# First GLU pass: product B11 of f tiles 1 to 13 by a nested seven-product scheme, and its background work placed anew

## The chip, the cores and the metric

The kernel runs on one core of a Trainium2 chip. The metric is device time in microseconds (us); the version before has a median of 2357.12 us over three runs (2354.83 to 2357.94). Engines: PE multiplies matrices, PEld is its weight load, DVE (vector), ACT (scalar) and POOL (GpSimd) work elementwise, SP issues DMAs. A row of the profile such as `L144 PE MATMUL` names the line of the kernel file that issued the instruction.

## What is computed

```python
x  = A_x                                  # 2048 x 1024, fp32
xn = layernorm(x)
q, k, v = split(xn @ wqkv)                # 1024 -> 3 x 1024, 32 heads of 32
phi(y) = concat(softmax(y @ w_phi), softmax(-(y @ w_phi)))    # per head
o  = phi(q) (phi(k)^T v) / (phi(q) sum(phi(k)) + 1e-6);  s = o @ wo
h  = sigmoid(xn @ w_gate) * (xn @ w_up)   # 1024 -> 3584, cut into 14 f tiles
out = x + s * silu(h @ w_down)
```

## The kernel before

**Products.** Each large product is cut in 2 x 2 and done with seven products instead of eight (a Strassen scheme in Winograd's form): B11, B21, B22 and T1 to T4 name the seven, and the sums of operand quarters that they need. An fp32 operand is split into a high and a low fp32r part by `split`: an ACT cast (L135) and a DVE subtraction (L136). `mm3` (L144 to L146) then issues three 128x512 matmuls, high by high, high by low and low by high, for one product of 128 rows of the contraction. A unit of work over one f tile ("glu op") fills PSUM banks 0 to 3 with 4 x 4 x 3 = 48 matmuls.

**The program order.** `ops` lists the work. The first projection chunk comes first, its opening written out by hand. GLU pass 0 follows: for each of 14 f tiles the ops B11 and B21, 28 of them. Then come the second projection chunk, GLU pass 1 (T2, T3, T4 of each f), pass 2 (T1, B22), the down product, and the attention with its output. The seven products of one f thus lie in three passes; between these, banks are copied out by ACT and kept in memory, and seeded or added again later.

**A nest.** In pass 2 the op T1 of f+1 is itself done by seven smaller products inside op B22 of f, for f = 1 to 12. `nest` fills banks 4 to 7 with six matmuls each for seven inner products (`product`), in place of 48, and between them runs the four quarters of the plain op (`plain`, 12 matmuls each, banks 0 to 3): 7 x 6 + 48 = 90 matmuls. Inner results pass from bank to bank by ACT: bank 4 to bank 5 (T2 adds to it), bank 5 to bank 6 (T3), bank 6 to bank 4 (T4). Bank 7 goes through a buffer in SBUF and is added by DVE (`added`). The finished quarters are added to what earlier passes left (`result`) and copied into banks 0 to 3, where the next plain op continues. The weights of a nest need four POOL sums of 128x256 (L530 to L533) and six splits instead of two, one of them half as large; `prep` does the splits ahead into a ring of eight slots, freed by `used()`.

**Background work.** `tick()` counts steps of the program and `later(n, f)` runs f at n ticks on: transfers, sums and normalisation for other stages. A glu op has one tick. `begin_pass` places the work: in pass 0 `x_stats`, `x_scales` and `x_rows` (the norm of the second half of x), four `x_pair` (they apply the norm by two 128x1024 DVE operations per `x_apply`, L849, and make POOL sums L254 and L290), and 16 `q_steps` (softmax of the query features: DVE L661, L662, L671, L672, L680, L681, and an ACT Exp of 128x1024, L675). Exp and the Sigmoid of the gate (L1425) use different ACT tables, so that an `ACT_TABLE_LOAD` stands ahead of each when they alternate. `wd_sums` are groups of four POOL sums of the down weights (L880 to L883): six groups in pass 1 (`WD_B`), four in pass 2 (`WD_C`). Instructions keep program order on each engine, so an instruction that waits holds up all behind it there.

**Attention in pass 1.** `kv_products` (L733) are small PE matmuls behind DVE's `k_low` (L727), which they follow by a fixed number of ticks.

Of the kernel before, what the change touches and what calls it, by code (L numbers as in the profile page):

```python
# [49 lines left out]
def hedgehog_glu_kernel(  # L50
# [103 lines left out]
    def later(n, f, *a):  # L154
        plan.setdefault(clock[0] + n, []).append((f, a))
# [15 lines left out]
    def tick():  # L171

        clock[0] += 1
        with behind():
            glu_group()
            nest_load()
            if not nests:
                glu_load(len(ops) - 1)
# [104 lines left out]
    xsets = (((53, 54), ((8, 9), (10, 11))), ((0, 1), ((2, 3), (26, 27))))  # L283
# [53 lines left out]
    o_split = Ring((54, 36, 37, 38))  # L337
# [38 lines left out]
    def folded(which, k, n, ps):  # L376
        f, r = FB[n][0], fraw[which][4 * k + n]
        for g in range(4):
            gs = slice(g * P, (g + 1) * P)
            nc.tensor.matmul(ps[:, gs], r[:, gs], bd[:, 4 * f + g], start=True, stop=True)  # L380
# [37 lines left out]
    ops += [("glu", 0, f, i) for f in range(NJ) for i in PASSES[0]]  # L418
# [10 lines left out]
    gr = Ring((41, 42, 39, 40))  # L429
# [4 lines left out]
    WD_B, WD_C = range(6), range(6, 10)  # L434
    last_raw, raw_free, spare, groups, made_sums = [], deque(), [], deque(), {}
    for f in FLY:
        groups.extend((f, s) for s in range(2))
        if 0 <= f - 4 < len(WD_B):
            groups.append((WD_B[f - 4], None))
    nests, nested = deque(k for k in range(1, NJ - 1)), {}  # L440

    def glu_load(n):
# [7 lines left out]
        if p == 0:  # L450
            r = gr.next()
            last_load[:] = [nc.sync.dma_start(whole(r), src).ins]
            wraw[n] = halves(r)
            return True
        if (p, f, i) == (1, 0, T2):
            raw_free.extend(halves(41, 42, 39, 40))
# [60 lines left out]
    def nest_load():  # L517

        if not nests or len(raw_free) < 6 or ops.index(("glu", 2, 1, T1)) not in wraw:
            return  # L520
        k = nests.popleft()
        ra, rb, rc, rd, gate, up = [raw_free.popleft() for _ in range(6)]
        for s, o in enumerate((ra, rb)):
            nc.sync.dma_start(o, wg_d[summed.index(T1), k + 1, :, s * HB:(s + 1) * HB])
        for s, o in enumerate((gate, up)):
            last_load[:] = [nc.sync.dma_start(o, wg_d[summed.index(B22), k, :, s * HB:(s + 1) * HB]).ins]
        lo, hi = slice(0, 256), slice(256, HB)

        def sums():
# [4 lines left out]
            nested[k] = rc, ra, gate, rb, rd, up  # L534
# [25 lines left out]
    def prep():  # L560
# [18 lines left out]
        if kind == "nest" and what not in nested:  # L579
# [3 lines left out]
        if kind == "nest":  # L583
            s = len(ready[n])
            src, cols = nested[what][s], slice(0, 256 if s == 4 else HB)
# [14 lines left out]
        if c:  # L600
            release(src)
# [201 lines left out]
    def x_stats(n):  # L803
        xt = x_load(CTT + n, xstat.next())
        later(5, x_moments, n, xt)
# [11 lines left out]
    def x_rows(q):  # L817

        rows = tps.next()
# [6 lines left out]
    def x_pair(u):  # L826

        xs, temps = xsets[u % 2]
        for th in range(2):
            n = 4 * th + u  # L830
            x_in(xs[th], temps[th], n)
            for w in range(2):
                later(4 + 2 * th + w, x_apply, xs[th], n, w)
            later(6 + 2 * th, x_keep, xs[th], temps[th], n, th, u)
            later(9 + 2 * th, outer_keep, n, temps[th])
        later(12, lambda: x_sums(halves(xs[0]), halves(xs[1])))
        later(15, lambda: x_sums_keep(u, halves(xs[0]), halves(xs[1])))

    def x_in(slot, temps, n):
        nc.sync.dma_start(whole(slot), xT[n])  # L840
# [10 lines left out]
    def x_keep(slot, temps, n, th, u):  # L851
# [6 lines left out]
        outer_sums(n, halves(slot), temps)  # L858
# [82 lines left out]
    qf_raw, qf_e = Ring(halves(36)), Ring((37, 38))  # L941

    def q_steps(at, t, hb):
# [16 lines left out]
        for n, f in ((0, load), (5, first), (6, lambda: spread(hold[2], *hold[:2])), (9, lambda: exponentials(hold[1])),  # L960
                     (11, sums), (13, keep)):
# [482 lines left out]
    def begin_projection(c):  # L1444
# [9 lines left out]
        for n in range(5):  # L1454
# [539 lines left out]
```

## Time and profile before

| | us |
|---|---|
| median of three runs | 2357.12 (2354.83 to 2357.94) |
| the profiled execution's own time | 2359.33 |
| its span, first to last instruction | 2357.5 |
| PE busy in the span | 2343.1 |
| DVE / ACT / POOL busy | 1651.5 / 1181.0 / 1056.9 |

| stage (us from the span's start) | length | PE | DVE | ACT | POOL busy |
|---|---|---|---|---|---|
| first projection chunk, 0 to 286 | 286 | 282.35 | 159.92 | 147.74 | 74.72 |
| GLU pass 0, 286 to 592 | 306 | 306.00 | 188.54 | 148.03 | 122.00 |
| second projection chunk, 592 to 821 | 229 | 229.00 | 185.88 | 127.02 | 36.63 |
| GLU pass 1 and the entry of pass 2, 821 to 1345 | 524 | 523.03 | 348.16 | 284.40 | 255.58 |
| GLU pass 2 with its nests, 1345 to 1580 | 235 | 231.69 | 145.63 | 117.99 | 176.59 |
| down product, 1580 to 2110 | 530 | 530.00 | 442.84 | 236.49 | 261.56 |
| attention and output, 2110 to 2357 | 247 | 241.04 | 180.57 | 119.33 | 129.82 |

The boundaries are cut by eye, at round numbers. How to read the rows shown further on: a row of the timeline gives the start, the duration, engine, line, operation, output and inputs, and in brackets the idle time of the engine ahead of it with what ended it. Matmuls overlap, so the step from one start to the next, not the duration, is what one costs. "xN" is a count; in groups, "busy, mean" are us and ns.

### The profile page before, as it was taken

The page shows a single profiled execution, that of the slowest core. Times are in us where ns is not written, and L with a number is a line of the kernel's source. Part 1 is how long each engine was busy: PE and PEld are TensorE (multiplying, and loading weights), DVE is VectorE, ACT ScalarE, POOL GpSimd, SP SyncE. Part 2 cuts the span into 40 slices and gives each one's busy share as a digit, 9 for nine tenths or more (in the row PEclk, how much of TensorE's full clock was granted, in tenths as well). Part 3 has the DMA queues.
Part 4 walks back from the last instruction along what each step waited for, and adds up shares of the span by engine and source line. Part 5 has one row for each costly group of instructions (what it writes and reads, how often), then busy time and mean ns, then how long its engine had stood idle before and what let it go on. Part 6 is the DMA issues. An engine that isn't in the chain of part 4 may idle for free.

```text
span 2357.5 us, 32347 instructions
## 1 busy us (share of the span) xinstructions
PE 2343.1 (99%) x10900; PEld 1954.7 (83%) x10900; DVE 1651.5 (70%) x2083; ACT 1181.0 (50%) x1848; POOL 1056.9 (45%) x737
## 2 busy tenths in 40 slices
PE   9999999999999999999999999999999999999999
PEld 8888888888888888888888888788888888888887
DVE  7625557755688856568776766565999888877776
ACT  7344544455644655555555555453444444355553
POOL 0323226731132035657622677784656443424566
PEclk9999999999999999999999999999999999999999
DMA  8789989986787786878874988789877667785665
GB/s 297 258 302 358 329 316 343 376 287 205 260 271 257 251 285 231 319 263 300 279 239 153 328 269 272 231 291 351 301 255 266 225 202 246 253 284 207 204 204 180
DMA packets 300406, 633.56 MB, mean 269 GB/s; under 512 B 38096, under 2 KB 38352, under 8 KB 295632
## 3 DMA queue, kind: packets, MB, share of 16 engines
q1 hardware_dynamic: 300240, 631.51, 77.2%
q8 instruction: 85, 1.39, 0.2%
q14 instruction: 81, 0.66, 0.1%
HBM read 378.40 MB, written 252.97 MB: 268 GB/s over the span
## 4 chain that ended last, share of the span: by engine, by line
PE 93%; DMA 3%; POOL 1%; DVE 1%; issue 1%; ACT 1%; SPq 1%; POOLq 0%; DVEq 0%
PE bank L144 29%; PE bank L145 29%; PE bank L146 29%; PE bank L733 1%; PE bank L1072 1%; PE bank L1048 1%; PE bank L380 1%; DMA fc<-e_d 0%; DMA fb<-wqkT 0%; DMA x<-x 0%; DMA wf_d<-p 0%; DMA fa<-wf_d 0%; DMA fc<-w_down 0%; DMA h_d<-x 0%; PE bank L248 0%
## 5 line engine op out<-in xcount | busy, mean ns | idle before, releaser
L144 PE MATMUL bank<-x,w 128*128 128x512 f32 x2304 | 896.7, 390 | 3.3 <-ACT bank L1560 3.3
L145 PE MATMUL bank<-x,w 128*128 128x512 f32 x2304 | 897.7, 390 | 0.0
L146 PE MATMUL bank<-x,w 128*128 128x512 f32 x2304 | 896.4, 389 | 0.0
L136 DVE TENSOR_TENSOR w<-fa,w 128x512 fp32r<-128x512 f32 (+1 forms) x383 | 372.2, 978 | 356.1 <-ACT w L135 343.5
L144 PEld LDWEIGHTS bank<-x,w 128*128 128x128 f32 x2304 | 432.9, 188 | 93.0 <-ACT bank L1560 3.7
L145 PEld LDWEIGHTS bank<-x,w 128*128 128x128 f32 x2304 | 433.0, 188 | 89.5 <-DVE x L136 0.3
L146 PEld LDWEIGHTS bank<-x,w 128*128 128x128 f32 x2304 | 432.9, 188 | 89.2
L135 ACT CAST w<-fa 128x512 fp32r<-128x512 f32 (+1 forms) x383 | 263.8, 691 | 420.8 <-PE bank L145 312.0
L144 PE MATMUL bank<-w,x 128*128 128x512 f32 x708 | 277.4, 392 | 0.0
L146 PE MATMUL bank<-w,x 128*128 128x512 f32 x708 | 276.0, 390 | 0.0
L145 PE MATMUL bank<-w,x 128*128 128x512 f32 x708 | 275.9, 390 | 0.0
L146 PEld LDWEIGHTS bank<-w,x 128*128 128x128 f32 x708 | 132.9, 188 | 27.8 <-DVE x L1248 0.3
L145 PEld LDWEIGHTS bank<-w,x 128*128 128x128 f32 x708 | 133.1, 188 | 26.1
L144 PEld LDWEIGHTS bank<-w,x 128*128 128x128 f32 x708 | 133.0, 188 | 26.2
L1392 ACT COPY fc<-bank 128x512 f32<-128x512 f32 x168 | 96.9, 583 | 96.5 <-PE bank L146 49.5
L136 DVE TENSOR_TENSOR w<-fb,w 128x512 fp32r<-128x512 f32 (+1 forms) x99 | 96.3, 979 | 65.1 <-ACT w L135 64.9
L135 ACT CAST w<-fb 128x512 fp32r<-128x512 f32 (+1 forms) x99 | 60.8, 615 | 119.6 <-PE bank L145 96.7
L136 DVE TENSOR_TENSOR x<-fb,x 128x512 fp32r<-128x512 f32 (+1 forms) x86 | 95.6, 1112 | 30.9 <-ACT x L135 29.3
L1086 POOL TENSOR_TENSOR fc<-fc 128x512 f32<-128x512 f32 x32 | 48.9, 1528 | 59.3 <-DVE fc L1081 23.9
L136 DVE TENSOR_TENSOR p<-fc,p 128x512 fp32r<-128x512 f32 (+1 forms) x67 | 49.3, 747 | 32.8 <-ACT p L135 30.2
L135 ACT CAST x<-fb 128x512 fp32r<-128x512 f32 (+1 forms) x86 | 68.2, 796 | 6.1 <-DMA fb<-w_down 2.9
L311 POOL TENSOR_TENSOR fb<-fb 128x512 f32<-128x512 f32 x6 | 9.2, 1525 | 133.7 <-DMA fb<-w_gu 133.7
(399 smaller groups left out, 3614.5 us busy)
## 6 DMA issues: line engine op xcount, KB each, us to landing
m_d<-fc SPq DMA_DIRECT2D x168, 256.0 KB, 3.9
fa<-h_d SPq DMA_DIRECT2D x147, 256.0 KB, 4.3
fa<-wf_d SPq DMA_DIRECT2D x32, 1024.0 KB, 6.4
x<-m_d SPq DMA_DIRECT2D x124, 256.0 KB, 4.9
h_d<-fc SPq DMA_DIRECT2D x104, 256.0 KB, 4.2
fc<-e_d SPq DMA_DIRECT2D x48, 512.0 KB, 5.8
fc<-qkv_d SPq DMA_DIRECT2D x72, 256.0 KB, 5.0
fa<-w_gu SPq DMA_DIRECT2D x60, 256.0 KB, 4.6
```

What stands on the lines that cost most here:

```text
L135: nc.scalar.copy(o[0], src)
L136: i = nc.vector.tensor_sub(o[1], src, o[0].bitcast(F32))
L144: nc.tensor.matmul(o, a[0], b[0], start=first, stop=False, **kw)
L145: nc.tensor.matmul(o, a[0], b[1], start=False, stop=False, **kw)
L146: last_mm[:] = [nc.tensor.matmul(o, a[1], b[0], start=False, stop=last, **kw).ins]
L311: nc.gpsimd.tensor_add(a22, a21, a22)
L380: nc.tensor.matmul(ps[:, gs], r[:, gs], bd[:, 4 * f + g], start=True, stop=True)
L733: nc.tensor.matmul(kvb[g // 2][:, g % 2 * 256:g % 2 * 256 + 256], v[:, g].rearrange("p a f -> p (a f)"), ph[:, g].rearrange("p a f -> p (a ...
L1048: nc.tensor.transpose(ps[:, j * P:(j + 1) * P], e[:, k * P:(k + 1) * P], ident)
L1072: nc.tensor.matmul(ps[:, j * 256:(j + 1) * 256], kg[:, k], ph[:, a, k], start=a == 0, stop=a == 1)
L1086: nc.gpsimd.tensor_sub(o, a, b)
L1392: nc.scalar.copy(o, banks[b])
```

## The change

- **Pass 0 uses nests.** Its ops become one glu op (B11 of f = 0), 13 nests, and one glu op (B21 of f = 13). The nest of f does B21 of f as the plain op and B11 of f+1 by seven inner products. `nest`, the nest's loads, sums and splits and the x operands of the inner products (`x_nest_load`, `x_nest_sums`, `x_nest_split`) take the pass as an argument. In pass 0 a finished quarter is copied twice by ACT: to a buffer that goes to memory (L1566) and to banks 0 to 3 (L1567). A nest has six ticks where the two ops it replaces had two.
- **The end of a nest moves.** The last quarter's results (`rest`) are issued in the next op, behind its first inner product and bank copy (`finish`); `result(1)` comes earlier. This holds for both passes.
- **Background work of pass 0 is placed by the nest's ticks.** `x_rows` transposes go into bank 7 at the start of nests f = 2 to 5, `x_pair` starts at ticks 18, 30, 42, 54 with temporaries shared between its two halves, 12 instead of 16 `q_steps` run in pass 0 (one every six ticks), and the other four in pass 2.
- **Other places.** All ten early `wd_sums` groups are in pass 1 and none in pass 2. `kv_products` run one tick later except at the last t of a half. Six instead of five `glu_sums` groups are in the second projection chunk, none in pass 0. Some buffers change their slots.

```diff
-    ops += [("glu", 0, f, i) for f in range(NJ) for i in PASSES[0]]
+    ops += [("glu", 0, 0, B11)] + [("nest", 0, f, B21) for f in range(NJ - 1)] + [("glu", 0, NJ - 1, B21)]
...
-    WD_B, WD_C = range(6), range(6, 10)
+    WD_B, WD_C = range(10), ()
...
-                     (9 + wide, k_inverses), (10 + wide, k_scale), (11 + wide, k_low), (13 + 2 * wide, kv_products)):
+                     (9 + wide, k_inverses), (10 + wide, k_scale), (11 + wide, k_low), (13 + 2 * wide + (t < TT - 1), kv_products)):
...
         if p == 0:
+            copies.items = halves(51, 50)
             for n in range(CTT):
-                later(1 + n + 4 * (n > 3), x_stats, n)
-            later(19, x_scales)
-            for q in range(4):
-                later(20 + q, x_rows, q)
+                later(1 + n + n // 4, x_stats, n)
+            later(14, x_scales)
             for u in range(4):
-                later(24 + 12 * u, x_pair, u)
-            for n in range(2 * CTT):
-                q_steps(2 + 13 * n // 2, n // 2, n % 2)
-            queue2(6, glu_sums, *sums.popleft(), halves(43, 44))
+                later(18 + 12 * u, x_pair, u)
+            for n in range(12):
+                q_steps(5 + 6 * n, n // 2, n % 2)
...
-                queue2(20 + 16 * n, wd_sums, j, halves(53, 54))
+                queue2(40 + 16 * n, wd_sums, j, halves(53, 54))
+            qf_raw.items, qf_e.items = [slots[50][:, 1]], [52]
+            for n in range(4):
+                q_steps(13 + 18 * n, 6 + n // 2, n % 2)
...
+    unfinished = []
+
+    def finish():
+        while unfinished:
+            unfinished.pop()()
...
-    def nest(n, f):
+    def nest(n, p, f):
...
-            h_added(1, f, ua, q)
+            if p:
+                h_added(1, f, ua, q)
+            else:
+                h_direct(0, f, q)
 
         def result(q, ps):
 
+            if not p:
+                o = copies.next()
+                nc.scalar.copy(o, ps)
+                nc.scalar.copy(banks[q], ps)
+                nc.sync.dma_start(m_d[0, f + 1, q], o)
+                return
...
         product(B11, a, True)
         nc.scalar.copy(b, a)
+        finish()
         plain(0)
         tick()
...
-        result(3, c)
-        result(1, b)
-        gated(1)
-        uvfree.extend(va[2:])
-        h_out(1, f + 1 + NJ, va[:2])
+
+        def rest():
+            result(3, c)
+            gate(1)
+            gated(1)
+            ...
+        unfinished.append(rest)
```

The line numbers move with the change. The three bank copies of a nest are L1592 (bank 4 to 5), L1600 (bank 5 to 6) and L1612 (bank 6 to 4) in the new file, a finished quarter's copies L1566 and L1567, bank 7's copy L1579, the gate's sigmoid L1429, Exp L677, the nest's weight sums L533 to L536, the `wd_sums` L884 to L887.

On PE, in the middle of pass 0. bank_101 to bank_104 are PSUM banks 0 to 3, bank_105 to bank_108 banks 4 to 7. Before, quarter 0 of a B21 op is followed by quarter 1:

```order
L144 MATMUL bank0_101<-x5_0_92,w_0_94 128x512
L145 MATMUL bank0_101<-x5_0_92,w_0_94 128x512
L146 MATMUL bank0_101<-x5_0_92,w_0_94 128x512
L144 MATMUL bank1_102<-x1_1_718,w_0_94 128x512
L145 MATMUL bank1_102<-x1_1_718,w_0_94 128x512
L146 MATMUL bank1_102<-x1_1_718,w_0_94 128x512
```

Now quarter 0 is followed by the inner product T2 on bank 5, which starts from what ACT copied there:

```order
L144 MATMUL bank0_101<-x5_0_92,w_0_94 128x512
L145 MATMUL bank0_101<-x5_0_92,w_0_94 128x512
L146 MATMUL bank0_101<-x5_0_92,w_0_94 128x512
L144 MATMUL bank5_106<-x2_2_2078,w_0_94 128x512
L145 MATMUL bank5_106<-x2_2_2078,w_0_94 128x512
L146 MATMUL bank5_106<-x2_2_2078,w_0_94 128x512
L144 MATMUL bank5_106<-x2_2_2078,w_0_94 128x512
L145 MATMUL bank5_106<-x2_2_2078,w_0_94 128x512
L146 MATMUL bank5_106<-x2_2_2078,w_0_94 128x512
L144 MATMUL bank7_108<-x3_1_1849,w_0_94 128x512
```

Six matmuls to bank 5 stand between quarter 0 and the next inner product, on bank 7.

On ACT, in pass 0, around an Exp. Before, it stands among the copies that keep B11 (L1392) and the two gates of a B21 op:

```order
L1392 COPY fc_100<-bank_103 128x512
L135 CAST w_94<-fa_97 128x2x512
L675 ACTIVATE p_0_96<-p_0_96 128x1024
L1392 COPY fc_100<-bank_104 128x512
L1425 ACT_TABLE_LOAD
L1425 ACTIVATE fb_99<-bank_101 128x512
L1425 ACTIVATE fb_99<-bank_102 128x512
```

Now it stands in the middle of a nest:

```order
L135 CAST w_94<-fa_97 128x512
L677 ACT_TABLE_LOAD
L677 ACTIVATE p_0_96<-p_0_96 128x1024
L1579 COPY fc_100<-bank_108 128x512
L135 CAST w_94<-fa_97 128x512
L1566 COPY fc_100<-bank_105 128x512
L1567 COPY bank_101<-bank_105 128x512
L135 CAST w_94<-fa_97 128x256
L1429 ACT_TABLE_LOAD
L1429 ACTIVATE fb_99<-bank_102 128x512
L1612 COPY bank_105<-bank_107 128x512
```

Between the Exp and the copy bank 6 to 4 on the last row, on which PE's product T4 depends, stand three more copies, two casts, a table load and a sigmoid.

At a nest's end, on DVE, the x_apply (L854) and the Exp's row sums (L682) of the background now stand ahead of the nest's last additions and gate products (fb_99, fc_100 and x are buffers in SBUF, stq the row statistics):

```order
L682 TENSOR_REDUCE stq_3268<-p_0_96 128x32
L854 TENSOR_TENSOR x_1_2163<-x_1_2163,x_2_2164 128x1024
L683 RECIPROCAL stq_3268<-stq_3268 128x32
L1580 TENSOR_TENSOR bank_107<-bank_107,fc_100 128x512
L1431 TENSOR_TENSOR fb_99<-fb_99,bank_103 128x512
L136 TENSOR_TENSOR w_94<-fa_97,w_94 128x512 x2
L1580 TENSOR_TENSOR bank_106<-bank_106,fc_100 128x512
L1431 TENSOR_TENSOR fb_99<-fb_99,bank_104 128x512
```

On ACT there, a cast, a finished quarter's copies and the copy bank 6 to bank 3, which waits for the L1431 on the last row above, stand ahead of the copy bank 4 to 5 (L1592):

```order
L135 CAST w_94<-fa_97 128x512
L1579 COPY fc_100<-bank_108 128x512
L1566 COPY fc_100<-bank_106 128x512
L1567 COPY bank_102<-bank_106 128x512
L135 CAST w_94<-fa_97 128x512
L1567 COPY bank_104<-bank_107 128x512
L1592 COPY bank_106<-bank_105 128x512
```

In that chain an addition (L1580), two copies, a product (L1431) and two more copies follow one another across the two engines.

On POOL, in the second half of pass 2. Before, a `wd_sums` group (L880 to L883) lies among the weight sums of a coming nest (L530 to L533), the gate's products (L1437, L1552) and the sums of h (L1408):

```order
L880 TENSOR_TENSOR fc_100<-fc_100 128x512
L881 TENSOR_TENSOR fc_100<-fc_100 128x512
L1437 TENSOR_TENSOR fc_100<-fc_100,x_3_9538 128x512
L882 TENSOR_TENSOR fc_100<-fc_100 128x512
L1552 TENSOR_TENSOR x_3_9538<-x_3_9538,fb_99 128x512
L530 TENSOR_TENSOR fa_97<-fa_97 128x256
L883 TENSOR_TENSOR fc_100<-fc_100 128x512
L1437 TENSOR_TENSOR fc_100<-fc_100,x_3_9538 128x512
L531 TENSOR_TENSOR fa_97<-fa_97 128x256
L532 TENSOR_TENSOR fa_97<-fa_97 128x256
```

Now, in the same part of the pass:

```order
L533 TENSOR_TENSOR fa_97<-fa_97 128x256
L534 TENSOR_TENSOR fa_97<-fa_97 128x256
L1441 TENSOR_TENSOR x_4_9767<-x_4_9767,x_3_9768 128x512
L535 TENSOR_TENSOR fa_97<-fa_97 128x256
L1584 TENSOR_TENSOR x_4_9767<-x_4_9767,fb_99 128x512
L536 TENSOR_TENSOR fa_97<-fa_97 128x256
L1441 TENSOR_TENSOR x_4_9767<-x_4_9767,x_3_9768 128x512
L1584 TENSOR_TENSOR x_4_9767<-x_4_9767,x_3_9768 128x512
```

The four `wd_sums` are gone from this place, and the weight sums follow one another with one gate product between them.

More of the change, by code (lines that the diff above doesn't have):

```diff
@@ L578, in prep @@
             glu_load(n + 1)
-        if kind == "nest" and what not in nested:
+        if kind == "nest" and n not in nested:
             return False
@@ L1585, in nest @@
         added(b, 1)
+        result(1, b)
         tick()
```

190 lines of the change are left out of this document (115 added, 75 removed).

## Prediction

> **What bounds the kernel now.** I read the page's busy times and its chain first, then PE's steps in the timeline, then all of PE's waits, then the stages by windows.
>
> ```profile
> PE 2343.1 (99%) x10900; PEld 1954.7 (83%) x10900; DVE 1651.5 (70%) x2083; ACT 1181.0 (50%) x1848; POOL 1056.9 (45%) x737
> PE 93%; DMA 3%; POOL 1%; DVE 1%; issue 1%; ACT 1%; SPq 1%; POOLq 0%; DVEq 0%
> 479.71 0.39 PE L146 MATMUL bank<-x,w 128*128 128x512 f32 x1
> ...
> 481.98 0.39 PE L144 MATMUL bank<-x,w 128*128 128x512 f32 x1
> ```
>
> PE is busy for 2343.1 of 2357.5 us and carries 93% of the chain. Ten steps lie between the two matmuls (481.98 - 479.71), so one costs 0.227 us, though its row says 0.39. A removed matmul is worth 0.227 us as long as nothing else makes PE wait. PE's waits are few; these are the largest by releaser, and the stage rows of pass 0 and of pass 2's nests (start to end, length, then busy time of PE, PEld, DVE, ACT, POOL, clock, DMA share, GB/s):
>
> ```profile
> PE bank L144 <- ACT bank L1560: 3.3, 1, 3.3
> PE bank L1322 <- POOL ident masks.py:199: 1.5, 1, 1.5
> PE bank L1048 <- DMA fc<-e_d: 1.4, 1, 1.4
> PE bank L733 <- DVE p L727: 1.0, 1, 1.0
> ...
> 286.00:592.00 306.00, 306.00 (x1360) 253.44 (x1359) 188.54 (x233) 148.03 (x199) 122.00 (x79) 1.00 0.86 308
> 1358.00:1573.00 215.00, 211.69 (x927) 174.82 (x926) 130.71 (x167) 106.57 (x195) 158.28 (x131) 0.99 0.78 261
> ```
>
> Pass 0 has no PE wait: its 306 us are 1344 matmuls of 128x512 and 16 transposes. Pass 2 shows what a nest is on the chip: one wait of 3.3 us in some eleven nests, though DVE is 61% busy there, ACT 50% and POOL 74%.
>
> **The change, term 1: fewer matmuls.** An f tile's B11 and B21 take 48 + 48 matmuls; a nest does both with 90. Thirteen nests save 13 x 6 = 78, and 78 x 0.227 = 17.7 us. A nest then lasts 90 x 0.227 = 20.4 us.
>
> **Term 2: pass 2's wait.** The rows are POOL, ACT and PE around it.
>
> ```profile
> 1497.20 1.30 POOL L880 TENSOR_TENSOR fc<-fc 128x512 f32<-128x512 f32 x1 [9.82 <-DMA fc<-w_down]
> ...
> 1507.91 0.74 POOL L532 TENSOR_TENSOR fa<-fa 128x256 f32<-128x256 f32 x1
> 1508.68 0.62 ACT L135 CAST w<-fa 128x512 fp32r<-128x512 f32 x1 [4.87 <-POOL fa L532]
> ...
> 1513.34 0.56 ACT L1560 COPY bank<-bank 128x512 f32<-128x512 f32 x1
> 1510.26 0.39 PE L146 MATMUL bank<-x,w 128*128 128x512 f32 x1
> 1513.95 0.80 PE L144 MATMUL bank<-x,w 128*128 128x512 f32 x1 [3.31 <-ACT bank L1560]
> ...
> 1517.69 0.39 PE L144 MATMUL bank<-x,w 128*128 128x512 f32 x1
> ```
>
> A `wd_sums` group held POOL for 9.82 us on a DMA; the weight sums queued behind it ended late, ACT's cast stood 4.87 us at the head of ACT's queue, and the bank copies behind it made PE late. From 1510.26 to 1513.95 one step took 3.69 instead of 0.23, and the next nine, 1513.95 to 1517.69, took 3.74 instead of 2.04: after the wait matmuls ran at nearly half rate. In all 3.46 + 1.70 = 5.2 us. The change has no `wd_sums` in pass 2, so POOL's DMA wait is gone there. What is late next is the four `q_steps` put in their place, priced in term 4. I take -5.2; if the wait comes back in another form, 0.
>
> **Term 3: the attention's wait in pass 1.** L733 waited 1.0 us, 1.1 us by its steps:
>
> ```profile
> 1077.75 0.39 PE L146 MATMUL bank<-x,w 128*128 128x512 f32 x1
> 1079.11 1.10 PE L733 MATMUL bank<-p,p 128*128 128x256 f32 x7 [0.97 <-DVE p L727]
> ```
>
> `kv_products` a tick later stands some 48 matmuls (10.9 us) further from L727, so -1.1. The matmuls behind this shorter wait kept their pace.
>
> **Term 4: what the nests of pass 0 may make PE wait for.** In pass 0 ACT and DVE get more to do in less time. The prices, from the groups by line of pass 0 (count, then busy, mean ns):
>
> ```profile
> L135 ACT CAST w<-fa 128x512 fp32r<-128x512 f32 (+1 forms) x52 | 34.0, 654 | 81.0 <-PE bank L145 76.8 <-DMA fa<-wv 2.3 <-DMA p<-qkv_d 1.9
> L1392 ACT COPY fc<-bank 128x512 f32<-128x512 f32 x56 | 32.4, 583 | 50.0 <-PE bank L146 31.2 <-issue 15.8 <-DMA h_d<-fb 2.4
> L136 DVE TENSOR_TENSOR w<-fa,w 128x512 fp32r<-128x512 f32 (+1 forms) x54 | 51.9, 963 | 87.0 <-ACT w L135 83.7 <-PE bank L822 3.2
> L680 DVE TENSOR_REDUCE stq<-p 128x32 f32<-128x1024 f32 x16 | 19.4, 1210 | 0.0
> L672 DVE TENSOR_TENSOR p<-stq,p 128x512 f32<-128x512 f32 x16 | 17.5, 1092 | 0.0
> L671 DVE TENSOR_TENSOR p<-p,stq 128x512 f32<-128x512 f32 x16 | 15.7, 980 | 0.0
> L849 DVE TENSOR_TENSOR x<-x,x 128x1024 f32<-128x1024 f32 x8 | 13.8, 1728 | 0.1
> L1427 DVE TENSOR_TENSOR fb<-fb,bank 128x512 f32<-128x512 f32 x20 | 13.6, 678 | 16.7 <-PE bank L146 16.5
> L662 DVE TENSOR_REDUCE stq<-p 128x16 f32<-128x512 f32 x16 | 10.8, 673 | 0.0
> 452.71 0.62 ACT L135 CAST w<-fa 128x512 fp32r<-128x512 f32 x1 [0.57 <-PE bank L145]
> 453.35 1.28 ACT L675 ACT_TABLE_LOAD   x1
> 454.65 1.06 ACT L675 ACTIVATE p<-p 128x1024 f32<-128x1024 f32 x1
> 455.72 1.28 ACT L1425 ACT_TABLE_LOAD   x1
> 457.02 0.60 ACT L1425 ACTIVATE fb<-bank 128x512 f32<-128x512 f32 x1
> 1511.81 0.57 ACT L1542 COPY bank<-bank 128x512 f32<-128x512 f32 x1 [1.51 <-DVE x L1541]
> 1512.30 0.63 ACT L1544 ACTIVATE x<-x 128x512 f32<-128x512 f32 x1
> 1512.83 0.59 ACT L1542 COPY bank<-bank 128x512 f32<-128x512 f32 x1
> ```
>
> *Load per nest.* ACT: 13 copies x 0.58, 5.5 casts x 0.62, two sigmoids x 0.60, two table loads x 1.28 and an Exp of 1.06 are 15.8 us of 20.4, or 77%. DVE: 5.5 splits x 0.96, two additions and two products x 0.68, two x_apply x 1.7 where there are any, and one q step (1.21 + 1.09 + 0.98 + 2 x 0.67 and a small reciprocal of some 0.3) are 16.3, or 80%. Neither is the bound as a sum, but their queues are in order and their copies stand between PE's inner products.
>
> *Copy bank 6 to 4 (L1612), 12 nests with an Exp.* The cast ahead of the Exp can begin when T1 frees its slot, 30 matmuls or 6.8 us into the nest. From the timeline's steps: cast 0.64, table 1.30, Exp 1.07, copy 0.50, cast 0.53, two copies 1.0, a half cast some 0.4, table 1.30, sigmoid 0.53, copy 0.57: 7.8 us, done at 14.7. T4 needs it after 66 matmuls, 15.0 us in. A cover of only 0.3 us: I take 0.1 us a nest, and for the range 0 to 1.
>
> *Copy bank 4 to 5 (L1592), 8 nests with x_apply.* From the last inner product (78 matmuls, 17.7) run a copy, an addition, two copies, then behind the last plain quarter (20.4) a product and two copies: 20.4 + 0.7 + 0.5 + 0.6 = 21.7, 1.3 us into the next nest, needed at 18 matmuls or 4.1. If an x_apply (1.7) and a split (0.96) fall ahead of the product or the addition, it is some 4.0; with each at its worst a further 1.5. I take 0.5 x 8 = 4, nearer the mean rows than the worst; ends 0 and 12.
>
> *One-off.* In the nest f = 2 a third table load (1.28), the copy of normed rows and the transposes into bank 7 come together: 1.5, ends 0 and 4. Entry, last nest and its loads, against the row of a 1 MB load
>
> ```profile
> fa<-wf_d SPq DMA_DIRECT2D x32, 1024.0 KB, 6.4
> ```
>
> which is due about 9 us after it is issued: 0.4, ends 0 and 2. Transfers as a whole are covered: counted from the issues, pass 0 moves about 3% fewer bytes in 6% less time, so some 318 GB/s where the row of pass 0 had 308.
>
> *POOL.* 13 x 4 weight sums at 0.74 (row L532) add 38 us to pass 0's 122, or 57% of 288; they are issued four ticks, some 13 us, ahead of their nest. In pass 1 four more `wd_sums` groups are 16 x 1.3 = 21 us; POOL has half of that stage free, and no PE wait there before came from POOL. The four q steps give pass 2 some 20 us of DVE and 14 of ACT in 235, in place of 21 on POOL. For both passes 0.5, ends -0.5 (the earlier `result(1)`) and 4. The `glu_sums` group moved into the second projection chunk costs nothing: POOL is idle there for most of the time.
>
> **Sum.** -17.7 - 5.2 - 1.1 = -24.0; new waits 12 x 0.1 + 4 + 1.5 + 0.4 + 0.5 = +7.6; together -16.4. Against the profiled execution's own 2359.33 this is 2342.9; the median of the runs is 2.2 lower, so I forecast 2340.5. With every lower end it is 2332, with every upper end 2367 or more, but these will not all come together.
>
> **Rivals.**
> - *All hidden.* The queues give way as in ten of eleven nests of pass 2: -24, 2333. For it speaks that pass 2 had no wait with POOL at 74%; against it, ACT at 77% instead of 50%.
> - *The wait in pass 2 stays.* An Exp with its two table loads (3.7 us on ACT) lengthens the same chain that L880 did. Then term 2 is lost: 2345.7. Against: only four nests have an Exp, and the cover at L1612 is larger without the double copies.
> - *The gain is eaten in pass 0.* Waits of 1.3 to 2.2 us a nest take back 17 to 29 us: 2350 to 2362, mostly within 0.2% (4.7 us) of before, which is about what a measurement can tell from no change.
> - *Slower: DVE's queue becomes the period.* With splits and x_apply at their contended durations (splits 1.5 instead of 0.96, x_apply 2.3, softmax steps a fifth longer) DVE needs 8.2 + 2.7 + 4.6 + 6 = 21.5 us per nest, above 20.4, and the ACT copies behind it slip each time. It decides from 24.0 + 4.7 = 28.7 us, or 2.2 us for each of 13 nests; at 2.7 us a nest the time is 2357.1 - 24 + 35 = 2368. For it: a split lasted up to 2.3 us beside POOL; against: POOL is at 57%, below pass 2's 74%, where the split's mean was 1.0. The rows, as min/median/max in pass 0, and the group in pass 2:
>
> ```profile
> L849 DVE TENSOR_TENSOR x<-x,x x8: 1155/1706/2318, 397.0 to 467.6; 128x1024 f32<-128x1024 f32 x8
> ...
> L136 DVE TENSOR_TENSOR w<-fa,w x54: 639/693/2349, 285.4 to 589.8; 128x512 fp32r<-128x512 f32 x50, 128x1024 fp32r<-128x1024 f32 x4
> ...
> L136 DVE TENSOR_TENSOR w<-fa,w 128x512 fp32r<-128x512 f32 (+1 forms) x40 | 40.8, 1022 | 29.4 <-ACT w L135 29.3
> ```
>
> *A rule against the change.* In the rows above the table load at 453.35 is followed by its Exp 1.30 us later, and the next load by its sigmoid 1.30 us later: nothing but the load stands between. If a switch held ACT as long again as the load itself does (another 1.28), the L1612 chain would be 2.6 us longer, past its cover by 2.3, and 12 x 2.3 = 28 us would go: 2357.1 - 24 + 6 + 28 = 2367. The rows speak against it, so it has a chance of 1%, within the slower cases. The Trainium skill ("ScalarE: Activation LUTs", What ACT_TABLE_LOAD costs) states such a price for every switch: about 1283 ns for the load and about 1380 ns of drain. The load agrees with the 1.28 of these rows; the drain is not to be seen in these rows.
>
> **How the numbers follow.** Forecast 0.48 (its own range 2336 to 2347), all hidden 0.20, pass-2 wait stays 0.14, eaten 0.12 (of which 0.02 still faster by over 0.2%, 0.09 same, 0.01 slower), slower 0.06. Faster 0.48 + 0.20 + 0.14 + 0.02 = 0.84, same 0.09, slower 0.07. Leaving out the slowest tenth and the fastest tenth, the range is 2331 to 2353.
>
> **What the profile would show.** Right: 78 fewer matmuls at steps of 0.227, pass 0 near 292 us, small PE waits on L1592 and L1612 in nests with an x_apply or an Exp, none at about 1510 in pass 2, none at L733. Wrong: waits of over 1 us on L1592 or L1612 in every nest, DVE over 95% busy in pass 0; a wait in pass 1 that POOL's weight or w_down sums release; or a step after a longer wait at half rate, which multiplies what it costs.

## The result, and the profile after

The changed kernel takes 2344.39 us (median of five runs, 2340.34 to 2347.08) against 2357.12 before; the ratio is 0.9948 (95% interval 0.993 to 0.9966), 12 to 13 us less. The forecast was 2340.5. The profiled execution is the quickest of the five, 2340.34 with a span of 2338.5, so against the profiled execution of before (span 2357.5) it shows 19.0 us.

The page's busy times after:

```profile
PE 2325.4 (99%) x10822; PEld 1939.5 (83%) x10822; DVE 1687.9 (72%) x2143; ACT 1252.6 (54%) x2000; POOL 1120.4 (48%) x797
```

PE's waits after, by releaser (total, times, longest):

```profile
PE bank L144 <- ACT bank L1612: 2.7, 1, 2.7
PE bank L144 <- ACT bank L1392: 2.2, 2, 1.7
```

The windows of pass 0, pass 1 and pass 2 after (start to end, length, busy time of PE, PEld, DVE, ACT, POOL, clock, DMA share, GB/s):

```profile
283.00:572.00 289.00, 289.00 (x1284) 239.08 (x1282) 207.92 (x264) 206.66 (x337) 162.20 (x125) 1.00 0.87 309
801.00:1326.00 525.00, 522.75 (x2388) 435.27 (x2387) 344.58 (x375) 281.22 (x438) 278.65 (x183) 1.00 0.81 280
1326.00:1562.00 236.00, 233.03 (x1017) 191.43 (x1016) 160.78 (x209) 131.37 (x229) 161.97 (x129) 0.99 0.76 253
```

Pass 0 is now 289 us, PE busy for all of it, with ACT at 72% and DVE at 72%. The waits on L1560 and L733 are gone; new ones are on L1612, in pass 2, and on L1392 (`seed`, which puts a stored bank back), in pass 1. Outside pass 0 both programs issue the same matmuls, so the start of the same matmul can be compared. The change of the time between two such marks:

| stretch (us, before) | change | what it holds |
|---|---|---|
| entry, 0 to 286 | -2.9 | all of it ahead of 186 us, where both programs issue the same instructions: the two executions differ |
| pass 0, to 592 | -17.5 | 78 matmuls (-17.7), 0.2 of longer steps around the transposes, no wait |
| second projection, to 821 | +0.1 | |
| pass 1, to 1345 | +1.6 | L733's wait -1.2; two seed waits with their slow restart +2.8 |
| pass 2, to 1580 | +0.4 | the old wait -4.9; a new one +5.3 |
| the rest | -0.7 | the same instructions behind the last nest: the two executions differ |

The new wait of pass 2 can be followed back in the timeline through five queues (POOL, SP, DVE, ACT, PE):

```profile
1521.85 0.74 POOL L533 TENSOR_TENSOR fa<-fa 128x256 f32<-128x256 f32 x1 [7.11 <-DMA fa<-wg_d]
...
1517.88 0.41 SPq L529 DMA_DIRECT2D fb<-wg_d  x1
1526.19 0.32 SPq L1408 DMA_DIRECT2D h_d<-x  x1
...
1531.46 0.43 SPq L951 DMA_DIRECT2D fc<-qkv_d  x1
...
1536.99 0.69 DVE L663 TENSOR_REDUCE stq<-fc 128x16 f32<-128x512 f32 x1 [5.61 <-DMA fc<-qkv_d]
...
1538.90 0.64 ACT L1439 ACTIVATE fb<-fb 128x512 f32<-128x512 f32 x1 [7.03 <-DVE fb L1437]
...
1541.88 1.06 ACT L677 ACTIVATE fc<-fc 128x1024 f32<-128x1024 f32 x1
...
1546.56 0.58 ACT L1612 COPY bank<-bank 128x512 f32<-128x512 f32 x1
...
1544.06 0.39 PE L146 MATMUL bank<-x,w 128*128 128x512 f32 x1
1547.19 0.50 PE L144 MATMUL bank<-p,w 128*128 128x512 f32 x1 [2.75 <-ACT bank L1612]
```

POOL's weight sums wait 7.11 us for their transfer, the gate's product behind them (L1441, done at 1526.17) is late, and its store (L1408) stands at the head of SP's queue from 1519.1 to 1526.2. Behind it the load of the fourth q step (L951) goes out at 1531.46. DVE reaches the step first and waits 5.61 us for it at the head of its own queue; the gate's sum L1437, an addition behind it on DVE, holds ACT for 7.03 us; then the Exp with its table loads, and only then the copy that PE needs. Seven matmuls at half rate follow; the profile's granted clock is 0.50 from 1547.84 to 1551.25.

### The profile page after: what moved, and what is told of

It is laid out like the page before. It is cut to its first block, busy times and chain, and to the rows that moved or that the text cites. A ratio compares the mean times of both kernels' runs of the same rounds, so it can differ in the third digit from the quotient of the medians.

```text
span 2338.5 us, 32642 instructions
## 1 busy us (share of the span) xinstructions
PE 2325.4 (99%) x10822; PEld 1939.5 (83%) x10822; DVE 1687.9 (72%) x2143; ACT 1252.6 (54%) x2000; POOL 1120.4 (48%) x797
## 4 chain that ended last, share of the span: by engine, by line
PE 95%; DMA 1%; DVE 1%; ACT 1%; POOL 1%; issue 1%; SPq 0%; POOLq 0%; DVEq 0%; ACTq 0%
PE bank L144 30%; PE bank L146 30%; PE bank L145 30%; PE bank L1076 1%; PE bank L735 1%; PE bank L1052 1%; PE bank L379 1%; PE bank L1326 0%; DMA wf_d<-p 0%; PE bank L247 0%; DMA fc<-e_d 0%; DMA wd_d<-fb 0%; DMA fc<-qkv_d 0%; DMA fb<-w_gu 0%; DMA wd_d<-fa 0%
## 5 line engine op out<-in xcount | busy, mean ns | idle before, releaser
L144 PE MATMUL bank<-x,w 128*128 128x512 f32 x2252 | 877.1, 390 | 2.5 <-ACT bank L1392 2.2
L145 PE MATMUL bank<-x,w 128*128 128x512 f32 x2252 | 877.0, 389 | 0.0
L146 PE MATMUL bank<-x,w 128*128 128x512 f32 x2252 | 875.9, 389 | 0.0
L136 DVE TENSOR_TENSOR w<-fa,w 128x512 fp32r<-128x512 f32 (+2 forms) x388 | 378.4, 981 | 324.2 <-ACT w L135 315.8
L144 PEld LDWEIGHTS bank<-x,w 128*128 128x128 f32 x2252 | 423.1, 188 | 91.2 <-ACT bank L1392 3.1
L146 PEld LDWEIGHTS bank<-x,w 128*128 128x128 f32 x2252 | 422.9, 188 | 87.7
L145 PEld LDWEIGHTS bank<-x,w 128*128 128x128 f32 x2252 | 423.1, 188 | 87.1
L135 ACT CAST w<-fa 128x512 fp32r<-128x512 f32 (+2 forms) x388 | 265.1, 685 | 333.7 <-PE bank L145 233.9
L136 DVE TENSOR_TENSOR w<-fb,w 128x512 fp32r<-128x512 f32 (+1 forms) x120 | 113.1, 947 | 67.6 <-ACT w L135 67.4
L135 ACT CAST w<-fb 128x512 fp32r<-128x512 f32 (+1 forms) x120 | 72.9, 609 | 115.4 <-PE bank L145 81.7
L1396 ACT COPY fc<-bank 128x512 f32<-128x512 f32 x116 | 66.7, 584 | 42.5 <-PE bank L146 20.6
L135 ACT CAST x<-fb 128x512 fp32r<-128x512 f32 (+1 forms) x83 | 63.0, 761 | 10.9 <-DMA fb<-xo_d 5.6
```

Of the source, the lines that this page charges most:

```text
L135: nc.scalar.copy(o[0], src)
L136: i = nc.vector.tensor_sub(o[1], src, o[0].bitcast(F32))
L144: nc.tensor.matmul(o, a[0], b[0], start=first, stop=False, **kw)
L145: nc.tensor.matmul(o, a[0], b[1], start=False, stop=False, **kw)
L146: last_mm[:] = [nc.tensor.matmul(o, a[1], b[0], start=False, stop=last, **kw).ins]
L1396: nc.scalar.copy(o, banks[b])
```

## The experiments

Two theories stood at the start: (A) the waits that remain come from the order of instructions that the change made, each from a part that can be named, and (B) they are chance, from when transfers land. Times are medians; ratios are against the kernel before, timed in the same set.

**The changed kernel again.** No edit.

> The changed kernel unchanged, as the base for this set. In its first trace PE waits after the entry at three places that the change touched: 0.7 and 1.7 us on the seed copies L1392 in pass 1, and 2.7 us on L1612 in pass 2 with seven matmuls at half rate behind it, some 7.6 us in all; none in pass 0. Theory A (the waits belong to the order of the instructions): they stand at the same places again, within 1 us each, and the time is 2344 within 4. Theory B (they are chance, from when transfers land): they move or vanish in another execution.

2345.42 us, 0.9943 (0.9929 to 0.9956). Its profiled execution has the wait on L1612 in pass 2 again (2.6 us) and a seed wait of 0.7; the first seed wait is missing and L1592 in pass 2 has 1.5. Pass 2 is as A says, pass 1 only in part.

**Pass 2 without q steps.**

```diff
+            if t in (4, 5):
+                nc.sync.dma_start(r_d[t + 2, hb], hold[3])
+                nc.sync.dma_start(e_d[t + 2, hb], hold[1])
...
-            for n in range(4):
-                q_steps(13 + 18 * n, 6 + n // 2, n % 2)
```

> The four q_steps of pass 2 are left out (no load, no softmax steps, no Exp; what they should store is filled by a second store of two earlier steps in pass 0, so the output for those rows is not the reference's). Theory A (the q step is what makes the copy L1612 late in pass 2): the 2.7 us wait and the half-rate matmuls go, 4.9 to 5.3 us less than the changed kernel, no wait on L1612. Rival C (the head of the chain is POOL, whose weight sums wait 7.1 us for a weight transfer there, and it is late without a q step too): a wait stays in pass 2, less than 1.5 us gained.

2337.16 us, 0.9914 (0.9901 to 0.9927): 8.3 us less than the changed kernel beside it, more than the 5.3 of the trace. No wait on L1612 is left. PE's largest waits (L1395 is the seed copy here):

```profile
PE bank L144 <- ACT bank L1395: 2.4, 2, 1.8
PE bank L1329 <- POOL ident masks.py:199: 1.5, 1, 1.5
```

Rival C falls: POOL's own wait for weights is still there (6.62 us ahead of L533 at 1514.54) and does not make PE late when no q step follows.

**The q loads earlier.** `q_early` issues the four loads eight ticks ahead. Its first load lands on a buffer that still holds part of an operand of the nests, so it does not compute the same output; `q_ahead` has that one a single tick ahead, and the other three eight.

```diff
-        for n, f in ((0, load), (5, first), ...
+        for n, f in ((-ahead, load), (5, first), ...
...
-                q_steps(13 + 18 * n, 6 + n // 2, n % 2)
+                q_steps(13 + 18 * n, 6 + n // 2, n % 2, 8 if n else 1)
```

> The loads of the four q_steps of pass 2 are issued eight ticks (some 27 us) earlier, all else as in the changed kernel. Theory A1 (the load is late because SP was held up by stores that wait for POOL, and DVE then stands 5.6 us at the head of its queue): the DVE wait on this load goes and with it PE's wait on L1612, 4.9 to 5.3 us less than the changed kernel. Rival A2 (the Exp with its two table loads, 3.7 us on ACT, is what does not fit): L1612 stays late, less than 1.5 us gained, although leaving the q steps out helps.

> As q_early, but the first of the four loads is issued one tick earlier only, and the other three eight, so that none lands on a buffer still in use: a kernel that computes the reference. Theory A1 (three of four loads late is what cost): the same as q_early within 2 us, 2337 to 2341, no PE wait on L1612 in pass 2. Rival: the whole pass 2 is chance, then 2344 to 2346 as the changed kernel.

`q_early` 2338.94, 0.9921 (0.991 to 0.9933); `q_ahead` 2337.81, 0.9913 (0.9898 to 0.9928). DVE's timeline in `q_early` at the place of the 5.61 us, then PE's waits of `q_ahead`:

```profile
1530.27 1.11 DVE L136 TENSOR_TENSOR w<-fa,w 128x512 fp32r<-128x512 f32 x1
1531.30 0.67 DVE L663 TENSOR_REDUCE stq<-fc 128x16 f32<-128x512 f32 x1
```

```profile
PE bank L144 <- ACT bank L1392: 2.9, 2, 1.5
...
PE bank L144 <- ACT bank L1592: 1.1, 2, 0.9
```

L663 runs without a wait, and L1612 is gone from PE's list although Exp and table loads stand at the same places in ACT's order. A1 holds, A2 falls: with its load in time the q step fits but for about 1 us at L1592. The median of `q_ahead` is below both kernels.

**Six down groups in pass 1.**

```diff
-    WD_B, WD_C = range(10), ()
+    WD_B, WD_C = range(6), ()
...
+                if j in (2, 3, 4, 5):
+                    nc.sync.dma_start(wd_d[i, j + 4], b)
```

> The down-weight groups 6 to 9 are not formed (their stores are filled with the sums of groups 2 to 5, so the output is not the reference's); pass 1 then has six groups as before the change, pass 2 none. Theory A (the four groups added to pass 1 make the weight sums, through them ACT and DVE, and so the seed copies late): the waits on L1392 go, 2.5 to 2.8 us less than the changed kernel. Rival D (the seeds are late from the attention steps moved a tick, or by chance): the waits stay.

2343.41 us, 0.9937 (0.9925 to 0.995), 2.0 less than the changed kernel beside it, with overlapping intervals. No seed wait is left. Pass 2 kept its waits (L1602 2.0, L1614 1.5, and 1.6 of the 2.9 us on L1594, which is L1592 in the changed kernel), and 1.1 us of L1594 fall in the first nest of pass 0, the only trace with a wait of this size there apart from `copies3`. So the verdict rests on the absent seed waits, not on the time.

**The down groups alone, and with kv_products.** Edits to the kernel before.

```diff
-    WD_B, WD_C = range(6), range(6, 10)
+    WD_B, WD_C = range(10), ()
...
-        if 0 <= f - 4 < len(WD_B):
-            groups.append((WD_B[f - 4], None))
+        if 0 <= f - 3 < len(WD_B):
+            groups.append((WD_B[f - 3], None))
...
+    (second kernel only) kv_products at 13 + 2 * wide + (t < TT - 1)
```

> The kernel before the change with one part of it alone: the four down-weight groups of pass 2 moved to pass 1 (ten there, none in pass 2). Theory A (they made pass 2's old wait, and in pass 1 make the seed copies late): no PE wait in pass 2's nests, 5.2 us less there, and 1.5 to 2.8 us of new waits on the seed copies in pass 1; 2.4 to 3.7 us below the kernel before. Rival D (the seed waits come from something else of the change): no new wait in pass 1, 5.2 us below. Rival C (pass 2's POOL is late from its own weight transfers): the wait in pass 2 stays, no gain.

> before_wd with one more part of the change: kv_products a tick later. In before_wd PE waited 0.6 us twice on L733 (1.5 us by its steps) and nowhere on the seed copies, in the changed kernel it is the other way round. Theory G (what PE gains at kv_products it gives back at the seeds, since these are paced by the weight sums of ten down groups and not by PE): no wait on L733, waits of 1 to 2.5 us in all on the seed copies L1388 near 1170 and 1210, the time within 2 us of before_wd (2353.6). Rival H (the seed waits come from pass 0's nests or another part of the change): no seed wait, 1.5 us less than before_wd.

`before_wd` 2353.59, 0.9983 (0.9974 to 0.9992); `before_wd_kv` 2352.23, 0.9974 (0.9965 to 0.9984). Between the same two matmuls pass 2 loses 5.2 us in both, as term 2 said. The page's waits of `before_wd` have

```profile
PE bank L733 <- DVE p L727: 1.2, 2, 0.6
```

and neither kernel has a seed wait. Theory A holds for pass 2 and falls for pass 1: the ten groups alone do not make the seeds late (rival D, with its 5.2 us). Theory G, that the time gained at `kv_products` is simply given back at the seeds, falls too, and H holds: `before_wd_kv` has ten groups and no wait at either place. One thing that differs is seen in the timeline near 1130 us of the changed kernel, on POOL, DVE, ACT and PE (DVE's L719 is L717 in the kernels made from before):

```profile
1128.87 1.61 POOL L886 TENSOR_TENSOR fa<-fa,fb 128x512 f32<-128x512 f32 x1
1130.56 2.17 POOL L887 TENSOR_TENSOR fa<-fa 128x512 f32<-128x512 f32 x1
...
1129.26 2.31 DVE L719 TENSOR_TENSOR fc<-fc,stk 128x1024 f32<-128x1024 f32 x1
1131.49 0.67 DVE L663 TENSOR_REDUCE stk<-fc 128x16 f32<-128x512 f32 x1
...
1131.66 1.05 ACT L720 CAST p<-fc 128x1024 fp32r<-128x1024 f32 x1 [3.62 <-DVE fc L719]
...
1142.88 1.29 POOL L482 TENSOR_TENSOR fb<-fb,fa 128x512 f32<-128x512 f32 x1 [10.15 <-DMA fc<-qkv_d]
...
1150.79 2.05 POOL L482 TENSOR_TENSOR fa<-fa,fb 128x512 f32<-128x512 f32 x1 [2.51 <-DMA fb<-w_gu]
...
1157.42 0.62 ACT L135 CAST w<-fa 128x512 fp32r<-128x512 f32 x1 [4.65 <-POOL fa L484]
...
1158.59 0.50 PE L144 MATMUL bank<-x,w 128*128 128x512 f32 x1 [0.57 <-ACT bank L1392]
```

The same row in `before_wd_kv`, then in `after_again` with POOL's sum beside it:

```profile
1147.53 1.22 DVE L717 TENSOR_TENSOR fc<-fc,stk 128x1024 f32<-128x1024 f32 x1
```

```profile
1129.48 1.21 DVE L719 TENSOR_TENSOR fc<-fc,stk 128x1024 f32<-128x1024 f32 x1
1129.71 2.15 POOL L885 TENSOR_TENSOR fa<-fa 128x512 f32<-128x512 f32 x1 [0.70 <-DMA fa<-w_down]
```

In the changed kernel a POOL sum of a down group (L886) is running when this DVE operation starts, and it takes 2.31 instead of 1.22 us. ACT's cast and bank copies, SP's stores behind them, the next weight loads and two groups of POOL's weight sums follow late, the second with a long first sum (L482, 2.05 instead of 1.29 us); then come the cast of the weights at 1157.42 and the seed. In `after_again`, the same program, a sum falls on the operation as well, but it starts 0.23 us behind it, since it waited 0.70 us for its transfer: the DVE operation is short, the sum is long instead, and PE does not wait near 1157.

The second seed wait, near 1195, is the larger one (1.7 us), and another chain leads to it. POOL, ACT and PE in the changed kernel:

```profile
1180.36 1.28 POOL L482 TENSOR_TENSOR fa<-fb,fa 128x512 f32<-128x512 f32 x1 [6.47 <-DMA fa<-w_gu]
...
1184.40 0.62 ACT L135 CAST w<-fb 128x512 fp32r<-128x512 f32 x1 [5.62 <-POOL fb L484]
...
1194.52 0.59 ACT L1392 COPY bank<-x 128x512 f32<-128x512 f32 x1 [4.96 <-DVE fb L1431]
...
1195.16 0.50 PE L144 MATMUL bank<-x,w 128*128 128x512 f32 x1 [1.68 <-ACT bank L1392]
```

POOL's weight sums wait for their transfer and the cast of the weights for POOL; an Exp stands behind the cast, its row sums and a short L719 (1.21 us) ahead of the gate's product L1431, and this product ahead of the seed. This wait is in all seven traces with pass 0's nests and ten groups at this tick (0.6 to 2.0 us by the steps), `after_again` included, and in none of the others. So the groups have a part in both waits, but the long L719 near 1130 is not what makes the second; why `before_wd` and `before_wd_kv`, with ten groups, escape it was not tested.

**kv_products back**, from one profiled execution.

```diff
-    (13 + 2 * wide + (t < TT - 1), kv_products)
+    (13 + 2 * wide, kv_products)
```

> The changed kernel with kv_products at their old tick. Theory A (the tick removed the wait): a wait of 0.5 to 1.5 us on L735 behind L729 near 1060 us comes back. Rival F (the wait went because POOL's work beside it changed, which had stretched DVE's operation to 2.3 us): no wait there.

PE's timeline at the place, then PE's waits on L735:

```profile
1059.69 0.39 PE L146 MATMUL bank<-x,w 128*128 128x512 f32 x1
1061.05 1.21 PE L735 MATMUL bank<-p,p 128*128 128x256 f32 x8 [0.97 <-DVE p L729]
```

```profile
PE bank L735 <- DVE p L729: 1.6, 2, 1.0
```

The old wait is back, and a second one beside it (1.6 us in all): A holds, F falls. The L719 near 1130 takes 2.3 us here too, but PE comes about 2 us later to the seeds and waits only 0.4.

**Three more copies in each nest of pass 0.**

```diff
-                nc.scalar.copy(o, ps)
+                for _ in range(4 if q == 0 else 1):
+                    nc.scalar.copy(o, ps)
```

> The changed kernel with three more ACT copies of 128x512 in every nest of pass 0, behind the inner product B21 (the first result is copied four times instead of once, to the same buffer). In the trace L1612 ended 0.50 us ahead of its use in the nests 1 to 11, 0.05 in nest 12 and 1.9 in nest 0. Theory A (pass 0 is free only by this 0.5 us): three copies are 1.5 us, so PE waits 1.0 us in each of eleven nests and 1.5 in nest 12, 12 to 13 us more than the changed kernel, 2356 to 2359. Rival E (ACT has slack elsewhere that takes it up, as 77% of the period suggests): less than 4 us more.

2359.15 us, 1.0005 (0.9995 to 1.0014): the whole gain is gone, 13.7 us against the changed kernel of the set before (2345.42). PE's waits, then PE's timeline in one nest:

```profile
PE bank L144 <- ACT bank L1613: 15.1, 12, 3.3
```

```profile
526.30 0.39 PE L146 MATMUL bank<-x,w 128*128 128x512 f32 x1
527.75 0.50 PE L144 MATMUL bank<-p,w 128*128 128x512 f32 x1 [1.07 <-ACT bank L1613]
```

Eleven nests wait some 1.1 us each, 1.4 with the slower steps behind the wait (the twelfth wait, 3.3, is pass 2's own). Nest 12, for which 1.5 was expected, has none; there a cast that stood ahead of the copy stands behind it now. Pass 0 is 15.1 us longer than in the changed kernel. E falls: ACT's idle quarter does not help a copy that stands in the chain.

**The down groups placed elsewhere, on top of q_ahead.** `q_ahead_late` has the groups' sums of pass 1 one tick later, with their stores and the return of their buffers. The other two have eight and six groups in pass 1 and the rest at the start of the down product; there part of the sums or of what they read is overwritten, so they do not compute the same output.

```diff
-        later(8, free)
+        later(9, free)                                                          # q_ahead_late
...
-        for n, f in zip((4, 7), wd_parts(j, b)):
+        for n, f in zip((5, 8) if j < 10 else (4, 7), wd_parts(j, b)):      # q_ahead_late
...
-    WD_B, WD_C = range(10), ()
+    WD_B, WD_C = range(8), ()                                               # q_ahead_wd8; range(6) in q_ahead_wd6
...
-    for n, j in enumerate(range(10, NJ)):
-        later(1 + 14 * n, wd_sums, j, halves(46, 38))
+    for n, j in enumerate(range(8, NJ)):
+        later(1 + 10 * n, wd_sums, j, halves(46, 38))                           # range(6, NJ) and 8 * n in q_ahead_wd6
```

> q_ahead with the down groups' POOL sums of pass 1 one tick later (2.7 us), their stores and the return of their buffers too; nothing is left out. Theory P (a group's sums fall on DVE's L719, which then takes 2.3 instead of 1.2 us, and through ACT and SP make the next weight sums and the seed copies late; so far the long L719 near 1130 and a seed wait near 1157 went together wherever kv_products is late): with the sums moved the L719 near 1130 takes about 1.2 us, no seed wait near 1157, and the time is 1 to 3 us below q_ahead (2337.8). Rival Q (ten groups are simply too much for POOL and SP in pass 1, wherever they stand): seed waits of 2 to 3 us in all stay, same time or above.

> q_ahead with eight instead of ten down groups in pass 1; groups 8 and 9 are formed at the start of the down product, where the last four are, at ten ticks' distance. Theory G: the seed waits of 2.0 to 3.2 us in pass 1 shrink to under 1.5; down product without new waits, so 0.5 to 2.5 us below q_ahead (2337.8). Rival: the down product waits for a late T2 sum, or the buffers turn up waits there, and the time is above q_ahead.

> q_ahead with six down groups in pass 1 and eight at the start of the down product, at eight ticks' distance. Theory G: no seed wait in pass 1 as in wd6, 2 to 3 us below q_ahead, 2335 to 2336. Rival: eight groups on one pair of buffers hold up SP and POOL in the down product, whose loads or sums then come late, and PE waits there for more than the 3 us gained.

`q_ahead_wd8` 2342.69, 0.9936 (0.9923 to 0.9948), and `q_ahead_wd6` 2344.6, 0.9941 (0.9928 to 0.9955), have both a higher median than `q_ahead`: the first has a single seed wait (1.3), the second none, but the down product now waits 3.5 and 2.6 us once for an ACT copy. The rivals hold there. `q_ahead_late` is 2339.04, 0.9926 (0.9913 to 0.994), not to be told from `q_ahead`; its L719 in DVE's timeline, then what is left of PE's waits in pass 1:

```profile
1134.89 1.21 DVE L719 TENSOR_TENSOR fc<-fc,stk 128x1024 f32<-128x1024 f32 x1
```

```profile
PE bank L735 <- DVE p L729: 0.3, 1, 0.3
```

As P says, the operation is short again and no seed wait is left. A sum of the group still falls on it (L884, 0.23 us behind its start), so it is short because it comes first; and as sums, stores and buffers moved together, this run does not separate the long operation from the stores in SP's queue. For the time P does not hold: the 1 to 3 us are not in the median.

Over all profiled executions with the row near 1130, a long one (2.3 us) with `kv_products` late goes with a seed wait near 1157 (0.25 to 1.5 us by the steps, six kernels), a short one with none (`after_again`, `wd6`, `before_wd_kv`, `q_ahead_wd6`, `q_ahead_late`); with kv early, a long one goes without (`kv_back`, `before_wd`). `after_again` is the changed kernel itself with a short one. So B has its part in pass 1: whether a sum or the operation starts first changes from execution to execution, in `after_again` by a transfer for which POOL waited 0.70 us. A long row alone is not enough: the rows near 1091 and 1110 take 2.31 and 2.12 us in the changed kernel, and no seed wait follows within 40 us of either.

## Why the prediction was right, point by point

- *Term 1 (-17.7):* pass 0 became 17.5 us shorter. Right.
- *Term 2 (-5.2, "what is late next is the four q_steps"):* the old wait went (-4.9 here, -5.2 alone in `before_wd`), and the q steps brought +5.3. This is the rival "the wait in pass 2 stays", given 0.14, in its outcome; its mechanism, the Exp with its two table loads on ACT, fell with A2. The step that failed was to price the Exp on ACT and not the load: the text said of q steps only what DVE and ACT run, while the load waits in SP's queue behind POOL's stores and DVE waits for it at the head of its queue. Without them, `no_q2` is at 2337.16; with early loads 2337.81.
- *Term 3 (-1.1):* -1.2. Right, and `kv_back` shows the tick as its cause.
- *Term 4, pass 0 (+7.1):* 0.2, and no wait. The L1612 chain was sized well, the L1592 chain not. The two copies and the matmuls that need them, in a nest of the changed kernel:

```profile
518.69 0.55 ACT L1592 COPY bank<-bank 128x512 f32<-128x512 f32 x1
...
520.77 0.39 PE L144 MATMUL bank<-x,w 128*128 128x512 f32 x1
...
523.46 0.62 ACT L135 CAST w<-fb 128x512 fp32r<-128x512 f32 x1 [0.51 <-PE bank L145]
524.10 1.28 ACT L677 ACT_TABLE_LOAD   x1
525.40 1.06 ACT L677 ACTIVATE p<-p 128x1024 f32<-128x1024 f32 x1
...
530.56 0.59 ACT L1612 COPY bank<-bank 128x512 f32<-128x512 f32 x1
...
531.65 0.39 PE L144 MATMUL bank<-p,w 128*128 128x512 f32 x1
```

  From the cast to the end of L1612 are 7.69 us (7.8 forecast), and 0.50 us lie ahead of T4 (0.3 forecast); it was 0.49 to 0.50 in each of the nests 1 to 11, and 0.05 in nest 12. L1592 ended 0.7 to 1.9 us ahead of T2, where an end about 4.0 us into the nest and a wait of 0.5 us in each of eight nests were taken; it ended at 2.2 to 3.5. The mistake was to add an x_apply and a split to the chain: the last x_apply of a nest ended 5.0 to 6.0 us ahead of the nest's end, and of the two only splits stood there. (The sum ahead of it slips as well: 20.4 + 0.7 + 0.5 + 0.6 is 22.2, not 21.7.) In pass 2 this copy does make PE wait, by 0.8 to 1.7 us between 1554 and 1563 in seven of the other traces; `no_q2`, without q steps, has no such wait.
- *Term 4, passes 1 and 2 (+0.5):* the seeds cost 2.8 us in this execution, 0.9 at the first and 2.0 at the second. The price of 16 POOL sums was compared with POOL's idle half. What they cost came from their place: at the first seed a sum that starts ahead of a DVE operation, at the second a chain that begins with a late weight transfer and goes with the number of groups; how the groups delay that transfer stays open.
- *The sum:* -16.4 against -19.0 between the profiled executions, of which -3.6 lie in parts that the change does not touch, and -12.7 between the medians. So the time came out near because two errors of opposite sign, 7 us too much in pass 0 and 8 us too little in passes 1 and 2, offset each other. That they did is luck. (By its own terms the forecast is 2340.7, and POOL's 57% is 56%.)
- *The other rivals:* "all hidden" is what happened in pass 0 alone. The slower one did not come, but `copies3` shows its price: some 1.1 us of ACT work past the cover in eleven nests takes the whole gain. (The split of 2.3 us that spoke for it was one of 128x1024; the longest of 128x512 in pass 0 took 1.85.) The rule on a drain behind the table load (the Trainium skill, "ScalarE: Activation LUTs", What ACT_TABLE_LOAD costs) does not hold here: in the nest above the Exp starts 1.30 us after its load, as before (1.29 to 1.36 over the 27 loads of pass 0), and with another 1.3 us at each load the cover of 0.5 would have been gone.

Why the median is 4 us above the profiled execution: eleven runs of the changed kernel spread over 2339.4 to 2347.8, the ten of `q_early` and `q_ahead` over 2335.2 to 2341.6. This fits a wait in pass 2 that is longer in other executions, but no profile shows one of those. A part lies in the entry: one matmul there, before any difference of the programs, starts between 183.0 and 186.1 us in the fourteen traces, with 183.0 in the profiled execution and a median of 185.0, so an estimate for this part is 2 us.

## What to carry to other kernels

Price a moved step by its first transfer as well as by its arithmetic: ask behind which stores the load queues, and which engine will stand at the head of its queue for it. Cover is counted along the chain that ends at the matmul, not as the engine's idle share: with ACT at three quarters, half a microsecond was all there was, and work beside the chain cost nothing while work in it cost its length beyond that. An engine that is half idle can still make another late, when its operation is running as the other's starts.

## What the runs showed of the hardware

- DVE's 128x1024 product with two operands in SBUF (L719, L717) takes 1.20 to 1.23 us when no POOL sum is running at its start (330 rows of the fourteen traces) and 1.69 to 2.34 when one is (118 rows). In 38 of the 330 a POOL sum starts during the product; the product keeps its time, and the sum ends 2.37 to 2.39 us after the product's start, as `after_again` shows above with 2.15 instead of 1.29 us. So the one that starts second waits. The reduction behind it (L663, one operand) keeps its 0.67 under the same POOL sum. The Trainium skill ("GPSIMD Engine Reference", Key points) says that the two engines share SBUF interfaces and contend where DVE reads two inputs from SBUF; these rows agree.
- A wait of PE was followed by half-rate matmuls after 2.75 us (the changed kernel) and after 2.0 us, but not after 2.6 us in `after_again` and never after the eleven waits of 1.1 us in `copies3`. The profile's granted clock is 0.50 in these stretches, for 3.41 us in the kernel before, the changed kernel, `wd6` and `kv_back`, and for 6.83 us in `copies3` and `q_ahead_wd8` after waits of 3.3 and 3.5 us; it stays 1.00 in `after_again`. `wd6` and `after_again`:

```profile
1543.59 0.78 PE L144 MATMUL bank<-x,w 128*128 128x512 f32 x1 [1.98 <-ACT bank L1602]
1544.17 0.63 PE L145 MATMUL bank<-x,w 128*128 128x512 f32 x1
```

```profile
1545.99 0.50 PE L144 MATMUL bank<-p,w 128*128 128x512 f32 x1 [2.59 <-ACT bank L1612]
1546.33 0.40 PE L145 MATMUL bank<-p,w 128*128 128x512 f32 x1
```

  So the slow stretch does not follow from the length of the wait alone.
